# Attention followed by an expert layer on one core: a new order for the first three attention units, unread matmuls, and an earlier third expert

## The chip, the cores and the metric

The kernel runs on one core of a Trainium2 chip. Such a core has four engines that compute (TensorE or PE, VectorE or DVE, ScalarE or ACT, GpSimd or POOL), a fifth that only issues transfers (SyncE or SP), and 16 DMA engines that all queues share. Each engine works through its own instructions in the order in which they stand in the program, and waits on semaphores where it needs another's result. The metric is the device time of one execution in microseconds; several executions are timed and the median is compared.

## What is computed

The reference, cut to what matters (B, H, S, D = 4, 8, 768, 64; 8 global and 96 local positions; 3072 tokens of 512, 8 experts, F = 1024):

```python
scores = scale * np.matmul(q, k.transpose(0, 1, 3, 2)) + bias   # bias = -slope[h] * distance
scores = np.where(is_global | is_local, scores, -1e9)
a = softmax(scores)
x = matmul(a, v).transpose(0, 2, 1, 3).reshape(B * S, H * D)
logits = x @ w_gate                        # one logit per token and expert
# pairs in falling order of logit: a token takes the expert if it has none yet and the expert is not full (384)
for e in range(8):
    out[assigned == e] = np.maximum(x[assigned == e] @ w1[e], 0) @ w2[e]
```

## The kernel before

**Attention** works on 8 units (half of the heads of one batch, four heads), each of two pairs, a and b. Only a band of 216 queries per block of 120 keys is computed, in seven blocks, which stand in three groups (`GROUPS`, L196). What is done to a unit `u` is cut into named steps, and `step` (L539) issues one. Their names are those of the lists, with the unit after the colon:

- KT0, KT1, QT0, QT1: VectorE transposes half of k or q in blocks of 32 (`blocks`, L276) into one of four buffers `tT`. When both halves are done, the load of a later unit follows on SP (q of u+2 or k of u+3) into one of five raw slots.
- KB: ScalarE copies most of a k half to `kA` (`kA_big`, L284); KS: GpSimd copies the rest. QO: ScalarE, in some places VectorE, copies a q half to `qT` (`qT_out`, L299).
- S0, S1, S2: TensorE's scores of a group (L335). The PSUM they write is used again by the next group, so they wait for the biases of the one before. S1 of unit 0 uses spare banks.
- BI0a to BI2b: VectorE adds the bias (`bias`, L342), two instructions a step. EX: ScalarE takes the exponential (L360). M0, M1: GpSimd adds the overlapping parts (`merge`, L365). AV0, AV1: TensorE multiplies with v (`attend`, L384). OT: ScalarE copies the result out. SU: TensorE's sums and logits (`sums`, L403). LT, GT, LS: VectorE and GpSimd finish sums and logits. TK, TO: rows of x are transposed back and scaled. WT: a piece of the weights of the first two experts is loaded (`weight_piece`, L316).

The order is written out by hand. `ORDER` (L528) is one period in which steps of up to four units stand interleaved, and it is run through under `manual_schedule`, in which every engine's order is the program's. Ahead of it stands a prologue of `steps(...)` lines (L613 to L657) for what can't follow the period: unit 0, most of unit 1, the constants (`consts_`) and the first loads. `done` keeps a step from being issued twice.

**Routing** (`routing`, L707) finds the experts' tokens in four rounds (`fast_round`, L770) and then the two lists of indices (`dispatch`, L846). In the gaps, rows of x that are left are transposed on TensorE (`rows`, L745), scaled on ScalarE (L507) and written to `x_tok` in DRAM on SP. `fill` (L729) issues matmuls that nobody reads. Weights of the later experts are loaded by `late_weights` (L692) from GpSimd: one piece at the start of the routing and one in each of three rounds, the others in the experts' loop. A piece is a whole w1 or w2, 1 MB.

**Experts** (`experts`, L1044): for each expert three slabs of 128 tokens are gathered (L1057), transposed (`load_x`, L1063), multiplied with w1 (`hidden`, L1075, ScalarE's relu at L1082) and w2 (L1107), copied from PSUM by VectorE (L1110) and scattered to `out` (L1111). Expert 0 does slab 0 by itself and slabs 1 and 2 together. Here the order within an engine is the scheduler's, save for what is pinned by `keep_in_program_order`.

## Time and profile before

| | us |
|---|---|
| median of 3 runs | 273.35 (271.0 to 273.55) |
| the profiled execution | 269.57 |
| its span, first to last instruction | 267.9 |
| PE busy | 232.1 (87%) |
| DVE, ACT, POOL busy | 150.5, 153.5, 153.3 (56 to 57%) |

A row of the timeline has start and duration in us, the engine, the line of the kernel, the operation, output <- inputs, shapes and the number of instructions merged into it, and in brackets how long the engine was idle before and what released it. The releaser is inferred, and can be wrong where a wait is for several things. PEclk is TensorE's granted clock as a share of 2.4 GHz; 0.5 is 1.2 GHz. In the page's slices it stands in tenths.

### The profile page before, as it was taken

How to read it: one execution, taken by the hardware profiler on the slowest of the kernel's cores; microseconds unless marked ns; L12 is line 12 of the kernel's file. 1: busy time of each engine (PE TensorE's matmuls, PEld its weight loads, DVE VectorE, ACT ScalarE, POOL GpSimd, SP SyncE). 2: the span in 40 equal slices, each digit the busy share in tenths (PEclk: the TensorE clock that was granted, in tenths of full speed). 3: DMA queues.
4: the chain of work that ended last, by engine and by line, in shares of the span. 5: the costliest groups of instructions: out<-in, count | busy, mean ns of one | idle time of the engine just before them, and what ended most of it. 6: DMA issues, size and time to landing. Idle time of an engine off the chain costs nothing. (4 is left out here: it accounts for less than half of the span.)

```text
span 267.9 us, 6769 instructions
## 1 busy us (share of the span) xinstructions
PE 232.1 (87%) x2681; PEld 164.4 (61%) x2681; DVE 150.5 (56%) x332; ACT 153.5 (57%) x304; POOL 153.3 (57%) x283
## 2 busy tenths in 40 slices
PE   0675599999998999999878888999999989999960
PEld 0654478888886888878657651956555545555520
DVE  3699678879998976564787772132321412323130
ACT  2549658999989999645678860525235051432500
POOL 6878734749585989968311004757565564741240
PEclk9997579999999999999999995899999999999995
DMA  6998976675455399990699991599999999330221
GB/s 246 339 356 214 269 291 190 151 225 125 134 111 111 56 183 206 191 216 7 97 180 220 241 299 48 109 218 244 243 267 240 268 238 303 131 138 36 84 91 37
DMA packets 49862, 49.22 MB, mean 184 GB/s; under 512 B 29344, under 2 KB 41376, under 8 KB 49824
## 3 DMA queue, kind: packets, MB, share of 16 engines
q0 software_dynamic: 15680, 26.22, 46.6%
q1 hardware_dynamic: 34144, 22.50, 30.4%
q8 instruction: 23, 0.38, 0.6%
q14 instruction: 15, 0.12, 0.1%
HBM read 56.05 MB, written 9.44 MB: 244 GB/s over the span
## 5 line engine op out<-in xcount | busy, mean ns | idle before, releaser
L1082 ACT ACTIVATE hT<-ph 128x384 bf16<-128x384 f32 (+2 forms) x72 | 32.6, 454 | 62.5 <-PE ph L1079 60.9
L335 PE MATMUL ps<-qT,kA 32*128 32x216 f32 (+2 forms) x864 | 47.9, 358 | 15.0 <-POOL wgx L635 9.3
L353 DVE SCALAR_TENSOR_TENSOR P<-Dm,ps 128x432 f32<-128x432 f32 x92 | 49.2, 595 | 13.9 <-PE ps L335 13.8
L335 PEld LDWEIGHTS ps<-qT,kA 32*128 32x128 f32 x864 | 40.6, 200 | 20.1 <-POOL wgx L635 9.3
L372 POOL TENSOR_TENSOR S<-P 128x576 f32<-128x576 f32 (+1 forms) x32 | 39.0, 1218 | 19.9 <-ACT P L360 14.8
L360 ACT ACTIVATE P<-P 128x864 f32<-128x864 f32 x48 | 42.6, 923 | 13.5 <-DVE P L353 12.7
L393 PE MATMUL po<-P,v 128*64 128x216 f32 (+6 forms) x576 | 43.3, 299 | 2.9 <-ACT P L360 2.7
L393 PEld LDWEIGHTS po<-P,v 128*64 128x64 f32 x576 | 36.0, 139 | 12.5 <-ACT P L360 3.4
L1111 POOL DMA_INDIRECT out_dram<-ot,ido x24 | 23.6, 984 | 28.5 <-DVE ot L1110 25.3
L1057 POOL DMA_INDIRECT xe<-x_tok,idi x24 | 23.3, 969 | 26.8 <-PE pw L732 18.6
L1110 DVE COPY ot<-po 128x512 f32<-128x512 f32 x24 | 16.4, 691 | 30.9 <-PE po L1107 24.4
L1107 PEld LDWEIGHTS <-hT 128*128 128x128 bf16 x192 | 18.2, 98 | 19.2
L1073 DVE COPY xT<-pxe 128x512 bf16<-128x512 bf16 x24 | 9.5, 422 | 35.8 <-PE pxe L1070 35.0
L507 ACT ACTIVATE x<-pw,ri 128x64 bf16<-128x64 f32 x112 | 24.6, 363 | 5.7 <-PE pw L492 5.4
L286 ACT COPY kA<-tT_k 128x720 f32<-128x720 f32 (+2 forms) x18 | 23.9, 1339 | 5.5 <-DVE tT_k L278 5.5
L1107 PE MATMUL po<-w_late,hT 128*128 128x512 bf16 x96 | 22.0, 379 | 0.0
L1079 PE MATMUL ph<-xT,w_late 128*128 128x384 bf16 x128 | 21.5, 326 | 0.0
L400 ACT COPY oT<-po 128x384 f32<-128x384 f32 x32 | 14.5, 477 | 11.8 <-PE po L393 11.8
L303 ACT COPY qT<-tT_q 128x768 f32<-128x768 f32 (+1 forms) x13 | 19.7, 1512 | 0.6 <-DVE tT_q L278 0.6
L278 DVE STREAM_TRANSPOSE tT_k<-w_early 128x768 f32<-128x768 f32 x16 | 15.3, 969 | 6.6 <-DMA w_early<-in_k_dram 3.5
L1079 PEld LDWEIGHTS <-w_late 128*128 128x128 bf16 x128 | 12.5, 98 | 8.7
L278 DVE STREAM_TRANSPOSE tT_q<-w_early 128x768 f32<-128x768 f32 x16 | 14.9, 944 | 0.2 <-DMA w_early<-in_q_dram 0.2
(166 smaller groups left out, 309.2 us busy)
## 6 DMA issues: line engine op xcount, KB each, us to landing
w_late<-in_moe_w_dram POOLq DMA_DIRECT2D x8, 1024.0 KB, 11.9
w_early<-in_k_dram SPq DMA_DIRECT2D x8, 768.0 KB
w_early<-in_q_dram SPq DMA_DIRECT2D x8, 768.0 KB
v<-in_v_dram SPq DMA_DIRECT2D x32, 180.0 KB
w_early<-in_moe_w_dram POOLq DMA_DIRECT2D x8, 512.0 KB, 8.9
w_last<-in_moe_w_dram POOLq DMA_DIRECT2D x4, 1024.0 KB, 12.6
x_tok<-x SPq DMA_DIRECT2D x2, 768.0 KB
x_tok<-x SPq DMA_DIRECT2D x2, 384.0 KB
```

The lines of the kernel that those rows point to most:

```text
L278: nc.vector.transpose(out=t, in_=raws[kind, u][:, :, 32 * g : 32 * g + 32])
L286: nc.scalar.copy(out=kAs[u % 2][:, g, i0:i1, 8:128].rearrange("p i (c j) -> p i c j", j=NJ), in_=t[:, i0 * NC5 : i1 * NC5, :].rearrange("p ...
L335: nc.tensor.matmul(at(a)[:, o : o + w], lhsT=kA[r, gd, i, :], rhs=qTt[r, gd, KT * i : KT * i + w], start=(gd == 0), stop=(gd == 1), skip_g ...
L353: nc.vector.scalar_tensor_tensor(out=Ps[n][:, 2 * g : 2 * g + 2, t, :], in0=W, scalar=-8.0 * slopes[2 * (n % NPAIR) + t], in1=st[:, 0 : 2 ...
L360: nc.scalar.activation(P, P, AF.Exp, scale=0.125)
L372: nc.gpsimd.tensor_tensor(out=to[:, :, :, 0:OV], in0=P[:, i0 : i0 + m, :, 0:OV], in1=P[:, i0 - 1 : i0 + m - 1, :, KT:QW], op=ALU.add)
L393: nc.tensor.matmul(po[n, bank][64 * t : 64 * t + 64, a - QB * bank : z - QB * bank], lhsT=v7[:, t, i, :], rhs=Ps[n][:, min(i, 5), t, a - q ...
L507: nc.scalar.activation(x[:, 2 * hf + i, 128 * jj + 64 * t : 128 * jj + 64 * t + 64], ps[:, i, 64 * t : 64 * t + 64], AF.Identity, scale=ri ...
L1079: nc.tensor.matmul(ph[:, 128 * t0 : 128 * t1], lhsT=w1_of(e)[:, kc, 128 * fc : 128 * fc + 128], rhs=xT_of[e][:, kc, t0:t1, :].rearrange("p ...
L1082: nc.scalar.activation(hT[:, fc, 128 * t0 : 128 * t1], ph[:, 128 * t0 : 128 * t1], AF.Relu)
L1107: nc.tensor.matmul(po, lhsT=hT[:, fc, 128 * t : 128 * t + 128], rhs=w2_of(e)[:, fc, :], start=(fc == 0), stop=(fc == NFC - 1))
L1111: s = nc.gpsimd.indirect_dma_start(out=out[:, :], out_offset=bass.IndirectOffsetOnAxis(ap=ido[:, TSLAB * e + t : TSLAB * e + t + 1], axis= ...
```

## The change

It does this:

- The prologue of `steps` lines is replaced by one list, `PROLOGUE`, which holds units 0 to 2, nearly all of 3 and parts of 4 and 5. From unit 4 the period is as it was.
- `warm(24)`: 24 matmuls of 128 x 512 in one accumulation group, whose result is not read, stand first on TensorE.
- The four `tT` buffers and one of the two `qT` buffers become parts of one tile, `arena`. After the last use, w1 and w2 of expert 2 are loaded into it, issued at step GTa of unit 6; there are then 10 late pieces for 12.
- In the routing two late pieces are issued (rounds 0 and 1) for four; one more comes between the gathers of experts 0 and 1.
- In `dispatch` the last rows of x come before the one-hot matrices are built, fills are put into one accumulation group per call, there are 4 + 6 + 8 + 6 of them for 4 + 2 + 8, and the matmul `pf` stands ahead of the last six.
- Expert 0 goes slab by slab, with its TensorE instructions pinned in program order. Of the last output slab ScalarE copies three quarters, VectorE one.

```diff
+    arena = wpool.tile([128, 2 * (4 * NJ * 32 + 2 * S_)], BF16)
+    w1_next = arena[:, 0:WL].rearrange("p (k f) -> p k f", k=NKC)
+    w2_next = arena[:, WL : 2 * WL].rearrange("p (k f) -> p k f", k=NFC)
...
-            t = ttp.tile([128, NJ, 32], FP32, tag="tT", name=f"tT_{kind}{u}_{g}")
+            m = 2 * NJ * 32 * (len(tTs) % 4)
+            t = arena[:, m : m + 2 * NJ * 32].bitcast(FP32).rearrange("p (j c) -> p j c", c=32)
...
+        PROLOGUE = (
+            "KT0:0 KS0:0 KT1:0 QT0:0 QT1:0 KB1:0 QO0:0 WT:1 KP0:0 KS1:0 QP1:0 KB0:0 KP1:0 C12:0 KT1:1 QP0:0 QO1:0 "
+            "KT0:1 KB1:1 KS1:1 QT0:1 WG:0 S0:0 QT1:1 S1:0 KB0:1 BI0b:0 BI0a:0 QO1:1 S2:0 EX0a:0 BI1a:0 QO0:1 "
+            "BI2a:0 KS0:1 EX1a:0 BI2b:0 EX0b:0 AV0a:0 EX2a:0 KT0:2 S0:1 C10:0 OT0a:0 KT1:2 BI0a:1 AV1a:0 EX2b:0 "
+            "C0:0 KB1:2 C11:0 BI0b:1 M0a:0 BI1b:0 OT1a:0 KS1:2 QT1:2 S1:1 KB0:2 EX1b:0 M1a:0 KS0:2 C15:0 BI1a:1 "
+            "C6:0 M0b:0 BI1b:1 QO1:2 SUa:0 AV0b:0 EX1a:1 S2:1 EX0a:1 QT0:2 QT1:3 QO0:2 BI2b:1 BI2a:1 C1:0 AV1b:0 "
...
+            "GTa:1 LTb:1 BI2a:3 EX1b:3 GTb:1 LTa:2 C14:0 LS:1 QO1:4 AV1b:2 EX1a:3 OT1b:2 KT1:5 TKa:2 KB0:5 M0a:3 "
+            "TOa:2 SUb:2 GTa:2 EX2a:3 BI2b:3 LTb:2 M1a:3 "
+        ).split()
+        VLOAD = {"S0:0": 1, "S1:0": 2, "S2:0": 3}
...
+        def warm(n):
+            i = len(warms) % 2
+            t = ps_t.tile([128, 512], FP32, tag=f"t{i}", name=f"warm{len(warms)}")
+            warms.append(t)
+            for m in range(n):
+                nc.tensor.matmul(t, lhsT=ones_bf, rhs=ones_bf.rearrange("p (o n) -> p o n", o=1).to_broadcast([128, 4, 128]),
+                                 start=(m == 0), stop=(m == n - 1))
...
+            elif k == "KP":
+                kA_big(0, int(op[2]), 0, 2)
+            elif k == "QP":
+                qT_out(0, int(op[2]), 0, 14, dve=op == "QP1")
...
-                qT_out(u, int(op[2]))
+                qT_out(u, int(op[2]), 0 if u else 14, dve=u < 2)
...
+                if n == 2 * NU - 4:
+                    nc.gpsimd.dma_start(w1_next, moe_w1[W_EARLY].rearrange("(kc p) f -> p kc f", p=128))
+                    nc.gpsimd.dma_start(w2_next, moe_w2[W_EARLY].rearrange("(fc p) d -> p fc d", p=128))
...
+            warm(24)
...
-            for _ in range(n):
-                pw = ps_d.tile([128, 512], FP32, tag="pk", name="pw")
-                nc.tensor.matmul(pw, lhsT=ident_bf, rhs=w1_early[:, 0, 0, 0:512], start=True, stop=True)
+            pw = ps_d.tile([128, 512], FP32, tag="pk", name="pw")
+            for i in range(n):
+                nc.tensor.matmul(pw, lhsT=ident_bf, rhs=w1_early[:, 0, 0, 0:512], start=(i == 0), stop=(i == n - 1))
...
-            if kk < len(ROUND_KS) - 1:
+            if kk < 2:
                 nc.gpsimd.tensor_copy(out=turn, in_=Xe[:, 0:1])
                 late_weights(False)
...
             rows(2)
             fill(4)
+            rows(2)
+            fill(6)
...
-                if q4 == 1:
-                    rows(2)
...
-            fill(2)
             pO = ps_d.tile([128, NCHUNK], FP32, tag="pr", name="pO")
             for c in range(NCHUNK):
+                if c % 6 == 0:
+                    fill(2)
                 nc.tensor.matmul(pO, lhsT=ohls[c // 6][:, :, c % 6], rhs=OH[:, :, c],
                                  start=(c == 0), stop=(c == NCHUNK - 1))
-            fill(8)
+            pf = ps_d.tile([1, CE], FP32, tag="pr2", name="pf")
+            nc.tensor.matmul(pf, lhsT=ones_bf[:, 0:1], rhs=Mf, start=True, stop=True)
+            fill(6)
...
-            late_weights(False)
             rows(2)
...
+            def first_hidden(hT, t):
+                for f2 in range(NFC // 2):
+                    if f2 == 2 and t + 1 < TSLAB:
+                        load_x(0, (t + 1,))
+                    ph = ps_h.tile([128, CAP], FP32, tag="ph")
+                    for j in range(2):
+                        fc = 2 * f2 + j
+                        for kc in range(NKC):
+                            pin(0, nc.tensor.matmul(ph[:, 128 * j : 128 * j + 128],
...
             gather(0)
+            if first:
+                late_weights()
             gather(1)
...
-                    hidden(0, hT, 0, 1)
-                    load_x(0, range(1, TSLAB))
-                    hidden(0, hT, 1, TSLAB)
+                    for t in range(TSLAB):
+                        first_hidden(hT, t)
...
+                    cuts = (0, DM) if e < N_EXP - 1 or t < TSLAB - 1 else (0, 3 * DM // 4, DM)
...
+                        copy = nc.vector.tensor_copy if hi == DM else nc.scalar.copy
```

## Rows read from the trace of the kernel before

**Rows 1.** The page's slices of 6.7 us: TensorE's granted clock in tenths

```profile
PEclk9997579999999999999999995899999999999995
```

**Rows 2.** Windows, one period of attention: stretch, length, busy us of each engine, clock, DMA

```profile
50.60:63.70 13.10, 12.99 (x235) 10.78 (x234) 10.73 (x22) 12.18 (x15) 8.66 (x18) 1.00 0.70 189
```

**Rows 3.** Timeline of TensorE, 8 to 70 us: scores of S0:0, S1:1, S2:1, S1:3, S0:4

```profile
9.32 3.26 PE L335 MATMUL ps<-qT,kA 32*128 32x216 f32 x32 [9.32 <-POOL wgx L635]
...
30.65 3.26 PE L335 MATMUL ps<-qT,kA 32*128 32x216 f32 x32 [2.95 <-DVE P L353]
...
37.53 1.96 PE L335 MATMUL ps<-qT,kA 32*128 32x216 f32 x48
...
59.11 1.74 PE L335 MATMUL ps<-qT,kA 32*128 32x216 f32 x32
...
68.12 1.98 PE L335 MATMUL ps<-qT,kA 32*128 32x216 f32 x32
```

**Rows 4.** Timeline of VectorE, 5 to 31 us

```profile
5.32 1.84 DVE L278 STREAM_TRANSPOSE tT_k<-w_early 128x768 f32<-128x768 f32 x2 [3.51 <-DMA w_early<-in_k_dram]
7.39 1.84 DVE L278 STREAM_TRANSPOSE tT_q<-w_early 128x768 f32<-128x768 f32 x2 [0.23 <-DMA w_early<-in_q_dram]
...
9.26 1.42 DVE L303 COPY qT<-tT_q 128x336 f32<-128x336 f32 x3
...
28.38 2.12 DVE L353 SCALAR_TENSOR_TENSOR P<-Dm,ps 128x432 f32<-128x432 f32 x4
```

**Rows 5.** Timeline of ScalarE, 7 to 11 us: copies of unit 0

```profile
7.19 0.62 ACT L286 COPY kA<-tT_k 128x240 f32<-128x240 f32 x1 [0.23 <-DVE tT_k L278]
8.40 0.77 ACT L303 COPY qT<-tT_q 128x336 f32<-128x336 f32 x1 [0.59 <-DVE tT_q L278]
9.08 2.00 ACT L286 COPY kA<-tT_k 128x480 f32<-128x480 f32 x2
```

**Rows 6.** Timeline of GpSimd, 121 to 129 us: the last units, a late piece's issue

```profile
121.64 1.01 POOL L372 TENSOR_TENSOR S<-P 128x384 f32<-128x384 f32 x1 [2.88 <-ACT P L360]
...
128.35 0.81 POOL L699 DMA_DIRECT2D w_late<-in_moe_w_dram  x1 [0.65 <-issue]
```

**Rows 7.** The tile x_tok: its writes (duration ns min/median/max, first and last start us)

```profile
L522 SPq DMA_DIRECT2D x_tok<-x x7: 359/360/467, 118.0 to 158.8; - x7
```

**Rows 8.** Windows of 1 us as in rows 2: DMA share and GB/s last

```profile
161.00:162.00 1.00, 0.89 (x3) 0.21 (x2) 0.15 (x1) 0.00 (x0) 0.00 (x0) 0.50 0.12 39
```

**Rows 9.** Timeline, 154 to 176 us: the routing's end and expert 0

```profile
154.55 1.68 PE L732 MATMUL pw<-w_early,ident_bf 128*128 128x512 bf16 x4
...
157.84 0.93 ACT L507 ACTIVATE x<-pw,ri 128x64 bf16<-128x64 f32 x4 [0.62 <-PE pw L492]
...
159.44 1.27 PE L901 MATMUL pO<-OH,ohl 128*128 128x24 f16 x24
...
160.55 5.08 PE L732 MATMUL pw<-w_early,ident_bf 128*128 128x512 bf16 x8
...
163.18 1.08 POOL L1057 DMA_INDIRECT xe<-x_tok,idi  x1 [18.62 <-PE pw L732]
...
166.32 0.58 PE L1070 MATMUL pxe<-ident_bf,xe 128*128 128x128 bf16 x4 [0.44 <-DVE fc L1039]
...
167.47 3.10 PE L1079 MATMUL ph<-xT,w_early 128*128 128x128 bf16 x32 [0.57 <-DVE xT L1073]
...
171.75 3.66 PE L1079 MATMUL ph<-xT,w_early 128*128 128x256 bf16 x32
```

**Rows 10.** Timeline, 180 to 260 us: expert 1's start, a stall, the last eviction

```profile
180.22 1.95 PE L1079 MATMUL ph<-xT,w_early 128*128 128x384 bf16 x11
...
219.82 0.77 PE L1070 MATMUL pxe<-ident_bf,xe 128*128 128x128 bf16 x8 [1.03 <-DMA xe<-x_tok,idi]
...
221.08 4.91 PE L1107 MATMUL po<-w_late,hT 128*128 128x512 bf16 x22
...
258.55 0.69 DVE L1110 COPY ot<-po 128x512 f32<-128x512 f32 x1 [1.04 <-PE po L1107]
```

More of the change, by code (lines that the diff above doesn't have):

```diff
@@ L625 @@
             load("k", 2)
-            steps("KT0 KT1")
-            for g in range(2):
-                kA_big(0, g, 0, 2)
-                kA_small(0, g)
-            steps("QT0 QT1")
-            qT_out(0, 0, 0, 14)
-            qT_out(0, 1, 0, 14, dve=True)
-            consts_(0, 2)
-            for t in range(2):
-                nc.gpsimd.tensor_scalar(out=wgx[64 * t : 64 * t + 64, :, 8 * t : 8 * t + 8],
-                                        in0=wg_sb[64 * t : 64 * t + 64], scalar1=LSCALE, scalar2=None, op0=ALU.mult)
-            consts_(11, 12, 13)
-            load_v(1)
-            steps("S0")
-            for g in range(2):
-                kA_big(0, g, 2)
-                qT_out(0, g, 14, 32, dve=True)
-            for g in range(2):
-                done.update([(f"KB{g}", 0), (f"KS{g}", 0), (f"QO{g}", 0)])
-            steps("BI0a BI0b EX0a")
-            load_v(2)
-            steps("S1")
-            steps("KT0 KS0", 1)
-            steps("BI1a BI1b")
-            consts_(14, 3)
-            steps("KB0", 1)
-            steps("EX1a")
-            steps("KT1 KS1 QT0", 1)
-            load_v(3)
-            consts_(1, 6)
-            steps("S2 BI2a EX2a M0a M1a")
-            qT_out(1, 0, dve=True)
-            done.add(("QO0", 1))
-            steps("QT1", 1)
-            steps("BI2b")
-            steps("KB1", 1)
-            qT_out(1, 1, dve=True)
-            done.add(("QO1", 1))
-            steps("EX0b AV0a OT0a AV1a OT1a EX1b EX2b M0b")
-            consts_(5, 10, 15, 16)
+            for o in PROLOGUE:
+                op, u = o.split(":")
+                if o in VLOAD:
+                    load_v(VLOAD[o])
+                step(op, int(u))
             it0 = 1 + stage["S0"]
@@ L670 @@
                     step(op, it - stage[op])
-            assert len(done) >= NU * len(ORDER), len(done)
+            assert all((o.split(":")[0], u) in done for o in ORDER for u in range(NU))
             while wpieces:
@@ L1034, in routing @@
             rows_out(d0, nc.vector)
[L1035 to L1037 removed]
+            pf = dispatch()
             fc8 = dap.tile([1, N_EXP], FP32)
```

81 lines of the change are left out of this document (47 added, 34 removed), and 6 rows, old and new, of the table PROLOGUE.

## The prediction

> **What bounds the kernel now.** I read the page first. Over the whole span TensorE is busy most, but the clock line has two dips, one around 20 to 40 us and one around 160 to 170 us, where the granted clock is 0.5, the lower of its two levels (1.2 GHz); elsewhere it is 2.4 GHz [rows 1]. So the span falls into stages with different limits, and each is read by itself.
>
> The windows come next. In a steady unit of attention TensorE is busy 12.99 of 13.10 us and ScalarE 12.18, at full clock: TensorE sets the pace there and ScalarE is close behind [rows 2]. What comes out of order in the first units is therefore not made up later, and what is gained there is kept to the end of attention.
>
> The timeline shows what the first units lose. TensorE's first scores S0:0 start at 9.32, S1:1 at 30.65 and S2:1 at 37.53, and from there to S0:4 at 68.12 it runs on with hardly a gap. At the lower clock 32 score matmuls take 3.26 us, at the higher one 1.74 [rows 3]; S0:0's 3.26 says that TensorE was at the lower one there too, where the clock line, which has only the changes, shows full clock. On VectorE the transposes, q copies and biases of these units follow each other almost without a gap: biases BI0a:1 and BI0b:1 end at 30.5, and S1:1, which needs the PSUM that they read, starts 0.15 us after [rows 3, 4]. VectorE's order sets this stage, with TensorE's clock on top. The routing is a chain of small steps that this diff touches only at its end; expert stage and tail are TensorE's.
>
> **The change part by part.**
>
> *1. The order of the first three units.* I walk VectorE's new queue with the old durations [rows 4]. A transpose is 0.92 us (1.84 for two), a bias step 1.06 (2.12 for two: four instructions), and a q copy goes by columns: 336 + 432 + 432 took 1.42, so 0.40, 0.51 and, for all 768, 0.91. The four transposes of unit 0 are where they were (until 9.23, since q lands at 7.39). Then: QO0:0, QP1:0, KT1:1, QO1:0, KT0:1, QT0:1, QT1:1 = 0.51+0.40+0.92+0.51+3x0.92 = 5.10; BI0b:0, BI0a:0 2.12; QO1:1 0.91; BI1a:0 1.06; QO0:1 0.91; BI2a:0, BI2b:0 2.12; KT0:2, KT1:2 1.84; BI0a:1, BI0b:1 2.12. Together 16.2 us from 9.26, so they end at 25.4 where they ended at 30.5.
>
> Does anything make VectorE wait in it? ScalarE now copies KB1, KP0, KB0, KP1, QP0 from 7.19 on: 1.00+0.62+1.00+0.62+0.77 = 4.0, so S0:0 starts at 11.2 instead of 9.3 [rows 5]. It ends at 12.9 (14.5 at the lower clock); BI0b:0 comes up at 14.4. S1:0 has banks of its own; S2:0 follows BI0a:0 (16.5) and ends at 18.4, and BI2a:0 comes up at 19.3. S0:1 follows BI2b:0 (21.5), ends at 23.2, and BI0a:1 comes up at 23.3. So at full clock each score is done just in time, and at the lower one each costs up to 1.5 us. The loads: q0 was there 2.07 us after k0's first use [rows 4], so k1 and q1, next in the queue, should be there at about 9.5 and 11.6 (estimated); they are wanted at 10.2 and 12.5. The loads that SP now issues earlier (q3, k4 ahead of v) have 5 us and more.
>
> S1:1 then starts at 25.5, 5.1 us earlier. Up to S2:1 TensorE has S1:1 1.74, a sums step of some 1.1 and an attend step of some 1.2, VectorE BI1b:0, QT1:2, BI1a:1, BI1b:1 = 4.1: S2:1 starts at 29.7 against 37.53, 7.8 earlier. (The old stretch of 6.9 us was those same TensorE steps at half clock.) From S2:1 to S0:4 both orders hold the same TensorE work, 30.6 us [rows 3]. I do not expect all 7.8 to last: the new list puts BI2b:3, for which S0:4 waits, behind LTa:2 and TOa:2, which wait for TensorE steps after S2:3, and ScalarE has under 1 us per unit to spare [rows 2]. I take 1.6 back, so 6.2; bounds 4.6 and 7.8. GpSimd's constants are only reordered, and its merges keep a lead of over 1 us on the sums. The arena replaces two pools with the same number of buffers: nothing.
>
> *2. The unread matmuls ahead of the scores.* 24 of 512 columns in one accumulation group. The nearest row is 22 matmuls of 512 columns in 4.91, 0.223 each [rows 10]; at half the clock 512 columns are 0.427 (worked out). They take 5.4 to 10.2 us from when `ones_bf` is written, and end before or about when S0:0 can start (11.2), so they cost nothing. What they buy is S0:0 at full clock, for which the walk has cover anyway, and a chance that the clock stays up. In the walk TensorE still has idle gaps of 1 to 2 us from 14.6 to 25, and the old trace shows the clock falling in such a patch. Price: between 0 and 4.4 us (S0:1 and S1:1 1.5 each, attend and sums some 1.4). Since the new queue is denser, I take 1.0. Part 1 and 2 together: 5.2 us earlier at the end of attention.
>
> A rule speaks against counting more. The Trainium skill, "TensorE: Matmul & The Clock Gate", Part 1, says that the ramp is worth under 1% of a typical kernel's span and that one should not fit to it, which here would be under 2.7 us. The rows show more: 1.52 us lost in S1:1 alone, and the clock line has some 13 us at the lower clock in that dip [rows 1]. By that rule I would take about 2 us off the gain (268.4); the rows are what I go by.
>
> *3. Third expert's weights in the last unit.* Two more issues on GpSimd, some 0.81 us each, land behind GTa:6, where GpSimd stood idle 2.88 us waiting for ScalarE [rows 6]: hidden. Their own wait, for the last readers of the arena (unit 6's scores, unit 7's copies), is over a unit earlier. Without that cover they would delay a merge by up to 1.7 us, of which the sums behind it have little to spare. In the routing two pieces of 1 MB remain of four.
>
> *4. The end of the routing.* The last write of x_tok is issued at 158.8, after the last four ACT copies end at 158.77; bytes hardly move after 161.2; the first gather starts at 163.18 [rows 7 to 9]. The last rows now come up before ACT has worked off the 32 before them, so its 0.62 us of idle time goes: 0.6. The transfer itself loses its competition: of the 2.4 us from issue to last byte I take 1.0 (0 to 1.9); the 2.0 us after the last byte stays. Gather 1.6 earlier. Beside it TensorE: pO started at 159.44; 1.27 for it, 14 fills and some 0.3 for pf. At 0.223 a fill it is done at 164.2, at 0.427 at 167.0; by the gather the transposes could start at 164.7, against 166.32 [rows 9]. I take 165.0: 1.3 earlier (+0.7 to -1.6).
>
> *5. Expert 0 by slabs.* From the first transposes to expert 1's first matmul it was 13.9 us [rows 9, 10]. The 96 matmuls of 128 columns stand against 32 + 32 wider ones (3.10 + 3.66). Half of the old first slab ran at the lower clock, 0.097 each; at the higher one a quarter of 0.223 would be 0.056 by columns [rows 9, 10]. So 5.4 to 9.3 us for 6.8: I take no change (-0.9 to +2.0). A weight issue now stands between gathers 0 and 1 on GpSimd; gather 1 is wanted 11 us later.
>
> *6. The last weights* start one piece earlier. There was one stall, 1.03 us at 219.8, on a gather [rows 10]. The same eight pieces still stand around it; I count nothing (1.0 either way).
>
> *7. The tail.* The last eviction took 0.69 us [rows 10]. Three quarters move to ScalarE beside the last eight short matmuls; the remaining quarter is some 0.2 to 0.3: 0.4 less (0 to 0.5).
>
> **Sum.** 5.2 + 1.3 + 0.4 = 6.9 us. The profiled execution took 269.57 (span 267.9 and 1.7 around it), so 262.7 there; the runs' median is 273.35, 3.8 above the profiled one, and I take the difference off that: 266.4. Own range, by the terms' bounds: 263 to 270.
>
> **The rivals.**
> *B, the clock falls and stays down in the first units.* The gaps speak for it, the denser queue against it. It costs 4.4 in place of 1.0, so attention ends only 1.8 earlier, and the routing's end and tail give perhaps 0.7: 270.9.
> *C, slower: the unread matmuls take their latency and not their columns.* For: the old fills did, 4 in 1.68 (0.42) and, at the lower clock, 8 in 5.08 (0.635) [rows 9]. Against: each of those began a new tile, and matmuls of one group go at 0.223. At 0.635 the 24 take 15.2 us, S0:0 slips from 11.2 to some 16.5 and BI0b:0 by 3.9, which leaves 1.3 of the 5.2; fourteen fills take 8.9, so expert 0's transposes start at 169.9, 3.6 later than before; the slabs at the lower clock add 1.0. With the tail it is 2.9 slower: 276.2. It turns the sign from about 0.53 us a matmul (6.9 us over 38 matmuls at the forecast's mean of some 0.35).
>
> **How the numbers follow.** Forecast 0.74, B 0.18, C 0.08. A measurement of this kernel can tell about 1%, 2.7 us: faster means under 270.6. The forecast gives 0.72 faster and 0.02 within; B lies across that bound, 0.06 and 0.12; C gives 0.01 within and 0.07 slower. Range 261.5 to 271.8: it takes in the forecast, a stall of 1.0 us saved beside its best bounds, and most of B.
>
> **What would show it.** Right: S0:0 near 11 us, S1:1 near 25.5, S2:1 near 30, S0:4 near 62; the granted clock at 1.0 from 25 us on; the end of attention 5 us earlier; DMA busy in the last unit and less so before the gather; first gather some 2 us after the last bytes and near 156.5. Wrong: a clock of 0.5 through 25 to 37 us (B); unread matmuls more than 0.45 apart, or TensorE still on fills when the first gather lands (C); VectorE idle before KT1:1 or QT0:1 (loads late); or the first expert's slabs taking over 9 us.

## The result, and the profile after

| | before | after |
|---|---|---|
| median, timed side by side, us | 272.33 (271.0 to 273.55, 4 runs) | 268.69 (266.75 to 270.22, 4 runs) |
| ratio, 95% interval | | 0.9871 (0.9825 to 0.9917) |
| the profiled execution, us | 269.57 | 268.25 |
| its span, us | 267.9 | 266.4 |
| mean granted clock | 0.945 | 0.974 |

The change makes the kernel 3.6 us faster (1.3%); 6.9 were forecast. The two profiled executions are only 1.5 us apart in span: the one of before took less than any timed run of before. So the rows below are read against each other for where time went, and the size of the gain is taken from the medians. A ratio here and below leaves out runs that took over 1.5% more than the kernel's fastest; for rows_first_from_1 that is three of six.

First the start. The page's line of the granted clock, in 40 slices and tenths, then the timeline: TensorE from 0 to 70 us (the unread matmuls; scores S0:0, S2:0, S1:1, S2:1; S0:3 in two pieces; S0:4) and ScalarE's first row copies behind the attention at 125.68:

```profile
PEclk9979999999999999999999998999999999999995
```

```profile
1.21 8.15 PE L566 MATMUL warm<-ones_bf 128*128 128x512 bf16 x24 [1.21 <-POOL ones_bf L71]
11.12 1.74 PE L341 MATMUL ps<-arena,kA 32*128 32x216 f32 x32 [1.77 <-ACT arena L309]
...
16.23 2.84 PE L341 MATMUL ps<-arena,kA 32*128 32x216 f32 x48 [1.91 <-DVE P L359]
...
24.38 2.50 PE L341 MATMUL ps<-qT,kA 32*128 32x216 f32 x32
...
29.13 1.96 PE L341 MATMUL ps<-qT,kA 32*128 32x216 f32 x48
...
46.62 1.36 PE L341 MATMUL ps<-qT,kA 32*128 32x216 f32 x19
48.84 1.00 PE L341 MATMUL ps<-qT,kA 32*128 32x216 f32 x13 [0.86 <-issue]
...
63.04 2.32 PE L341 MATMUL ps<-arena,kA 32*128 32x216 f32 x32
...
125.68 1.75 ACT L513 ACTIVATE x<-pw,ri 128x64 bf16<-128x64 f32 x8 [1.92 <-PE pw L498]
```

The wide dip at 20 to 40 us [rows 1] is gone. S1:1 comes 6.3 and S2:1 8.4 us earlier than in [rows 3], S0:4 only 5.1. In between, S0:3 loses 1.5 us: 3.22 from start to end where 32 such matmuls take 1.74, with a gap of 0.86 us behind its 19th matmul for which the trace names no other engine ("issue"). The row copies came at 129.87 before: the attention ends 4.2 us earlier.

Windows of the lapse of the clock that is left there (stretch, length, busy us of PE, PEld, DVE, ACT, POOL, clock, DMA share, GB/s), and of a second one in expert 0. The DMA share adds up the times of all packets, so it can pass 1:

```profile
16.00:17.00 1.00, 0.77 (x16) 0.80 (x20) 1.00 (x3) 0.88 (x1) 0.00 (x0) 1.00 0.99 406
17.00:18.00 1.00, 1.00 (x24) 1.00 (x20) 1.00 (x3) 0.15 (x2) 0.38 (x1) 0.57 1.03 424
18.00:20.00 2.00, 2.00 (x29) 1.66 (x24) 1.52 (x3) 1.63 (x2) 1.10 (x1) 0.50 1.05 423
20.00:21.00 1.00, 1.00 (x14) 0.72 (x12) 1.00 (x3) 0.77 (x1) 0.56 (x2) 0.73 0.98 260
...
164.00:167.00 3.00, 3.00 (x31) 3.00 (x29) 0.42 (x1) 1.17 (x4) 2.39 (x4) 0.50 0.94 146
```

The end of the routing and expert 0, from the timeline (last write of x_tok, the last fills, first gather, expert 0's transposes, its first and last matmuls with w1, expert 1's start):

```profile
153.88 0.36 SPq L528 DMA_DIRECT2D x_tok<-x  x1
...
157.70 1.47 PE L740 MATMUL pw<-w_early,ident_bf 128*128 128x512 bf16 x6
...
158.52 1.08 POOL L1066 DMA_INDIRECT xe<-x_tok,idi  x1 [23.48 <-DVE fm L1050]
...
162.26 0.38 PE L1079 MATMUL pxe<-ident_bf,xe 128*128 128x128 bf16 x4 [3.09 <-issue]
...
163.22 1.26 PE L1094 MATMUL ph<-xT,w_early 128*128 128x128 bf16 x16 [0.57 <-DVE xT L1080]
...
171.34 0.61 PE L1094 MATMUL ph<-xT,w_early 128*128 128x128 bf16 x8 [0.88 <-issue]
...
178.46 5.36 PE L1104 MATMUL ph<-xT,w_early 128*128 128x384 bf16 x32
```

Against [rows 7, 9]: last write 4.9 us earlier, first gather 4.7, transposes 4.1, but expert 1 [rows 10] only 1.8. Expert 0 takes 16.2 us for 13.9. TensorE has done its fills at 159.2 and stands 3.1 us until the transposes of the first rows at 162.3, 3.7 us after their gather's start (2.9 to 3.2 in all other kernels here); behind that its clock falls. The first late piece asked for behind the first gather, in the kernel before (first line) and in the changed one, then in the changed one the stall ahead of expert 5, expert 5's start, and the tail:

```profile
170.55 0.85 POOL L699 DMA_DIRECT2D w_late<-in_moe_w_dram  x1
```

```profile
162.16 0.87 POOL L707 DMA_DIRECT2D w_late<-in_moe_w_dram  x1
...
218.49 0.77 PE L1079 MATMUL pxe<-ident_bf,xe 128*128 128x128 bf16 x8 [1.46 <-DMA xe<-x_tok,idi]
...
224.50 5.36 PE L1104 MATMUL ph<-xT,w_late 128*128 128x384 bf16 x32
...
256.79 0.48 ACT L1141 COPY ot<-po 128x384 f32<-128x384 f32 x1 [4.26 <-PE po L1138]
257.24 0.29 DVE L1141 COPY ot<-po 128x128 f32<-128x128 f32 x1 [1.05 <-PE po L1138]
258.30 0.97 POOL L1142 DMA_INDIRECT out_dram<-ot,ido  x1 [0.87 <-DVEq L1162]
```

So of 4.7 us at the first gather 1.5 are left at the end. Two questions follow: why the gather came at 158.5 and not near 156.5, and why what lies behind it became 3.2 us longer.

### The profile page after: what moved, and what is told of

It is laid out like the page before. It is cut to its first block, busy times and chain, and to the rows that moved or that the text cites. A ratio compares the mean times of both kernels' runs of the same rounds, so it can differ in the third digit from the quotient of the medians.

```text
span 266.4 us, 6908 instructions
## 1 busy us (share of the span) xinstructions
PE 236.4 (89%) x2745; PEld 167.1 (63%) x2755; DVE 149.4 (56%) x332; ACT 153.5 (58%) x301; POOL 152.6 (57%) x282
## 4 chain that ended last, share of the span: by engine, by line
PE 65%; DMA 11%; DVE 11%; issue 5%; ACT 4%; POOLq 1%; POOL 1%; DVEq 0%; ACTq 0%
PE ps L341 15%; PE po L399 14%; PE po L1138 11%; PE ph L1104 8%; DMA xe<-x_tok,idi 5%; DMA w_last<-in_moe_w_dram 5%; PE t L416 4%; PE ph L1094 3%; DVE P L359 3%; ACT x L513 2%; DVE arena L281 2%; PE pw L740 2%; PE t L420 2%; DMA w_early<-in_k_dram 2%; PE pxe L1079 2%
## 5 line engine op out<-in xcount | busy, mean ns | idle before, releaser
L1107 ACT ACTIVATE hT<-ph 128x384 bf16<-128x384 f32 x56 | 27.5, 491 | 51.7 <-PE ph L1104 50.0
L1141 DVE COPY ot<-po 128x512 f32<-128x512 f32 (+1 forms) x24 | 16.2, 675 | 32.6 <-PE po L1138 29.7
L281 DVE STREAM_TRANSPOSE arena<-w_early 128x768 f32<-128x768 f32 x32 | 29.8, 953 | 5.0 <-DMA w_early<-in_k_dram 3.6
L289 ACT COPY kA<-arena 128x720 f32<-128x720 f32 (+2 forms) x18 | 23.7, 1345 | 5.9 <-DVE arena L281 5.8
L341 PE MATMUL ps<-arena,kA 32*128 32x216 f32 (+2 forms) x416 | 21.7, 343 | 5.4 <-DVE P L359 2.5
L341 PE MATMUL ps<-qT,kA 32*128 32x216 f32 (+2 forms) x448 | 24.1, 335 | 2.0 <-DVE P L359 1.0
L341 PEld LDWEIGHTS ps<-arena,kA 32*128 32x128 f32 x416 | 18.7, 194 | 7.7 <-issue 5.0
L341 PEld LDWEIGHTS ps<-qT,kA 32*128 32x128 f32 x448 | 20.0, 184 | 4.6 <-issue 2.5
L406 ACT COPY oT<-po 128x384 f32<-128x384 f32 x32 | 14.7, 476 | 11.6 <-PE po L399 11.5
L1138 PE MATMUL po<-w_late,hT 128*128 128x512 bf16 x69 | 15.9, 379 | 0.0
L416 PE MATMUL t<-S,onesx 128*32 128x192 f32 x256 | 13.7, 332 | 0.0
```

What stands on the lines that cost most here:

```text
L281: nc.vector.transpose(out=t, in_=raws[kind, u][:, :, 32 * g : 32 * g + 32])
L289: nc.scalar.copy(out=kAs[u % 2][:, g, i0:i1, 8:128].rearrange("p i (c j) -> p i c j", j=NJ), in_=t[:, i0 * NC5 : i1 * NC5, :].rearrange("p ...
L341: nc.tensor.matmul(at(a)[:, o : o + w], lhsT=kA[r, gd, i, :], rhs=qTt[r, gd, KT * i : KT * i + w], start=(gd == 0), stop=(gd == 1), skip_g ...
L416: nc.tensor.matmul(pr[32 * gq : 32 * gq + 32, :], lhsT=onesx[:, t, :], rhs=S[:, t, 192 * gq : 192 * gq + 192], start=(t == 0), stop=True, ...
L1107: nc.scalar.activation(hT[:, fc, :], ph, AF.Relu)
L1138: pin(e, nc.tensor.matmul(po[:, lo:hi], lhsT=hT[:, fc, 128 * t : 128 * t + 128], rhs=w2_of(e)[:, fc, lo:hi], start=(fc == 0), stop=(fc == ...
```

## The experiments

Each kernel was timed beside the kernel before, whose medians ranged from 269.1 to 272.3 with the chip and the hour; so ratios and places in the trace are compared, and medians only between kernels that ran together. "To the end" is from the first gather to the end of the span; spans and places are of the profiled executions. Six kernels have the same program up to the end of the attention (changed, e0_whole, third_late, tiny16, rows_first_6, best_tiny); their first row copies behind it came between 123.9 and 125.7 us, the changed kernel's last of all. So a place in a single trace is uncertain by about 1 us either way.

| kernel | ratio (95%) | span | first gather | expert 1 | expert 5 | to the end |
|---|---|---|---|---|---|---|
| before | 1 | 267.9 | 163.18 | 180.22 | 225.83 | 104.7 |
| changed | 0.9871 (0.9825 to 0.9917) | 266.4 | 158.52 | 178.46 | 224.50 | 107.9 |
| e0_whole | 0.9833 (0.9788 to 0.9878) | 265.2 | 157.33 | 175.33 | 223.11 | 107.9 |
| no_warm | 0.9769 (0.9722 to 0.9817) | 264.1 | 156.31 | 174.34 | 222.03 | 107.8 |
| old_order | 0.9960 (0.9927 to 0.9992) | 268.7 | 160.69 | 179.05 | 226.69 | 108.0 |
| third_late | 0.9885 (0.9830 to 0.9940) | 266.6 | 158.56 | 179.37 | 224.67 | 108.0 |
| tiny16 | 0.9898 (0.9870 to 0.9926) | 264.9 | 156.73 | 173.18 | 222.94 | 108.2 |
| no_warm_tiny24 | 0.9911 (0.9885 to 0.9937) | 267.0 | 156.93 | 174.64 | 225.05 | 110.1 |
| no_warm_w_after | 0.9940 (0.9919 to 0.9962) | 266.3 | 155.93 | 172.36 | 224.24 | 110.4 |
| no_warm_whole_w | 0.9919 (0.9889 to 0.9949) | 266.0 | 156.46 | 172.30 | 223.95 | 109.5 |
| rows_first_6 | 0.9979 (0.9945 to 1.0013) | 268.9 | 157.77 | 181.49 | 226.96 | 111.1 |
| rows_first_from_1 | 0.9706 (0.9645 to 0.9766) | 262.1 | 154.65 | 172.78 | 218.07 | 107.4 |

### The start: the order and the unread matmuls

**old_order** puts the prologue's old lines back and keeps the rest.

```diff
-            for o in PROLOGUE:
-                ...
+            steps("KT0 KT1")
+            ...
```

> The changed kernel with the order of the first units as it was (unread matmuls kept). Theory: the new order is worth the attention's 4 to 5 us: S2:1 goes back to 36 to 37.5, the last sums end 4 to 5 us later, and the kernel is 3.5 to 5 us slower than the changed one, so some 1 us slower than the one before. Rival: the start sets only part, since the later units wait for VectorE anyway (S1:5 and S1:4 stood 0.6 to 1.0 us on it): 1 to 2.5 us slower.

S2:1 starts at 35.59 (6.5 later than in the changed kernel), S0:4 at 66.18 (3.1 later), the row copies at 127.96 (2.3 later), and the span ends 2.3 later. S2:1 in the trace shows the start; what remains of it at the end of attention is the rival's 1 to 2.5. Against the mean of the six kernels with the new order and the unread matmuls (124.8) the row copies are 3.2 later. So the order is what makes most of the kernel's gain (0.9960 without it, 0.9871 with it), but half to two thirds of its 6.5 us are lost again before the attention ends.

**no_warm** leaves out the unread matmuls.

```diff
-            warm(24)
```

> The changed kernel without the 24 unread matmuls ahead of the first scores. Theory (the prediction's step 2): they lie in time that TensorE has free and bring S0:0 to full clock; without them S0:0 starts near 11 and takes 3 to 3.5 us instead of 1.74, S2:1 starts 0 to 1.5 later, the kernel is 0 to 1.5 us slower. Rival: they delay the first scores and buy the lapse of the clock at 17 to 20.5 us, so that without them S2:1 is not later and the kernel is 0.5 to 2 us faster.

It is faster, and by more than the rival said: 0.9769 against 0.9871. TensorE's timeline (S0:0, S2:0, S1:1, S2:1, S0:3) and GpSimd's first gather in this kernel:

```profile
11.02 3.26 PE L341 MATMUL ps<-arena,kA 32*128 32x216 f32 x32 [11.02 <-ACT arena L309]
16.66 1.96 PE L341 MATMUL ps<-arena,kA 32*128 32x216 f32 x48 [0.79 <-DVE P L359]
...
24.26 2.50 PE L341 MATMUL ps<-qT,kA 32*128 32x216 f32 x32
29.01 1.96 PE L341 MATMUL ps<-qT,kA 32*128 32x216 f32 x48
...
45.96 1.74 PE L341 MATMUL ps<-qT,kA 32*128 32x216 f32 x32
...
156.31 1.08 POOL L1065 DMA_INDIRECT xe<-x_tok,idi  x1 [21.82 <-PE pw L739]
```

S0:0 takes 3.26 instead of 1.74, and nothing follows from it: S1:1 and S2:1 start 0.1 us *earlier*, because VectorE sets the scores ahead of them. The lapse at 17 to 21 us isn't there either: five of the six kernels with the new order and the unread matmuls have a stretch at 0.5 somewhere between 11.6 and 20.9 us (e0_whole has none), none of the six without them has. The gap in S0:3 is gone. It stands behind the same 19th matmul in all six kernels that have the new order and the unread matmuls (0.30 to 0.86 us), and there in none of the six that have the new order without them; S0:4 starts 1.2 us later with them (mean of six 62.3 against 61.1). In each of the six it ends 2.6 to 2.8 us after a packet of the instruction queue starts (what that is comes in the next section). Two of the other six have such a gap further on (no_warm 0.37 us up to 56.74, no_warm_tiny24 0.79 up to 49.77), 2.7 and 2.9 us behind such a packet. That fits TensorE waiting for its own instructions; no run tests it. By the row copies the 1.2 us are levelled out (124.8 against 124.6). The rows where no_warm really gains are at the gather: its last write of x_tok goes out at 153.32, so the gather follows it by 2.99 us, for 4.64 in the changed kernel; the other 0.6 us of the 2.2 are the earlier write.

### The first gather: a packet of the instruction queue

The DMA traffic of that stretch, GB/s in 40 slices of 0.15 us each from 153 to 159 us: the changed kernel, then no_warm.

```profile
GB/s 103 27 20 0 0 0 0 0 0 0 0 48 410 348 328 307 287 21 0 0 0 14 7 14 7 27 20 21 0 0 0 0 0 0 0 0 0 0 0 0
```

```profile
GB/s 0 0 0 0 0 0 0 0 287 348 341 341 335 96 0 0 0 0 0 0 0 0 0 109 0 0 0 0 0 0 0 0 0 0 300 109 300 164 0 0
```

In the changed kernel the last x_tok transfer has a tail: its last 17 packets come one by one, the last of them 1.5 us after the rest. In no_warm there is no tail; a single packet (109) stands alone at 156.5. The DMA view by queue names it. Queue, packets, MB, share of 16 engines; the changed kernel at 154.75 to 155.0, then no_warm at 156.5 to 156.75:

```profile
q8 instruction: 1, 0.02, 34.6%
```

```profile
q8 instruction: 1, 0.02, 30.6%
```

It is one packet of 16 KB of some engine's instructions, and it takes 1.2 to 1.4 us of one DMA engine (0.31 to 0.35 of 16 engines for 0.25 us). In the changed kernel it falls on the transfer's start. The Trainium skill, "Runtime: NRT & Kernel Launch", "Instruction fetch mechanics", says that each engine's instructions are fetched in blocks of 16 KiB, 256 instructions, by DMA, and that a block's cost is mostly hidden. The packet's size agrees; that it is hidden doesn't hold here. By the size of a block, 24 matmuls with their weight loads, 48 instructions, would move such a packet along TensorE's program. Two kernels test that, with 16 or 24 matmuls of 8 columns (two instructions each) in the routing rounds, where TensorE waits (tiny16 as below; no_warm_tiny24 with `tiny(6)` and without `warm(24)`):

```diff
+        def tiny(n):
+            pw = ps_d.tile([128, 512], FP32, tag="pk", name="pw")
+            for i in range(n):
+                nc.tensor.matmul(pw[:, 0:8], lhsT=ident_bf, rhs=ident_bf[:, 0:8], start=(i == 0), stop=(i == n - 1))
...
                                     start=(k1 == 0), stop=(k1 == k - 1))
+            tiny(4)
```

> The changed kernel with 16 unread matmuls of 8 columns added, four in each of the four routing rounds, where TensorE waits for VectorE. They add 32 instructions to TensorE's stream and nothing that anything waits for. Theory: the changed kernel's first gather starts 4.64 us after the issue of the last x_tok (2.95 without the unread matmuls at the start) because one 16 KB packet of the instruction queue falls into that transfer at 154.8 us, and 16 or 17 packets of x_tok come 1.5 us behind the rest; where that packet falls follows TensorE's place in its instructions. With 32 more instructions ahead it falls before the transfer: the gather starts 2.7 to 3.2 us after the last issue and the kernel is 1 to 2 us faster than the changed one. Rival: the gather waits for the reductions behind the dispatch (its releaser by the profile, fm), which nothing here moves: 4.3 to 4.9 us as before, the same time plus or minus 0.5.

> The changed kernel without the 24 unread matmuls at the start, and 24 unread matmuls of 8 columns in the routing rounds (six in each): at the dispatch TensorE's stream has as many instructions behind it as in the changed kernel. Theory (the packet of the instruction queue): it falls into the last x_tok transfer again, the first gather starts 4.3 to 4.9 us after the last issue, and of the 3.2 us that leaving out the unread matmuls gained 1 to 2 are lost (266.5 to 267.5). Rival: the whole gain is of the start (clock, the gap in S0:3): the gather 2.7 to 3.2 us after the last issue, 265.0 to 266.2.

The same GB/s line from 152 to 158 us, tiny16 and then no_warm_tiny24:

```profile
GB/s 355 246 34 0 0 0 0 109 0 0 0 0 0 198 314 355 348 335 123 14 27 20 14 0 0 0 0 0 0 0 0 0 0 0 0 0 0 0 0 0
```

```profile
GB/s 0 0 0 0 205 423 335 348 321 116 0 0 0 0 0 0 7 7 7 14 7 27 20 21 0 0 0 0 0 0 0 0 0 0 0 0 0 0 0 0
```

In tiny16 the packet (109) has moved ahead of the transfer, and only a short tail is left right behind the transfer; in no_warm_tiny24 it is back on top of the transfer, with the tail. From the last write's issue to the first gather:

| packet | kernels | us |
|---|---|---|
| behind the transfer | no_warm, no_warm_w_after, no_warm_whole_w, rows_first_from_1, best_cold | 2.99 each |
| ahead of it (16 small matmuls) | tiny16, best_tiny | 3.62, 3.68 |
| on it, or on its end | changed, old_order, rows_first_6, no_warm_tiny24, e0_whole, third_late | 4.5 to 5.2 |

The releaser that the timeline prints (fm, in the rival) was wrong: nothing about fm was moved. In all 14 traces the gather starts 1.2 to 1.3 us after the last packet of that write has ended; it waits for the write. The kernel before is no exception: there, too, such a packet stands in the write (at 161.05, the 130 in its GB/s line from 158 to 164 us, slices of 0.15 us), and the write's last packet ends at 161.98, behind a tail:

```profile
GB/s 423 341 382 341 376 342 396 369 396 287 219 369 362 389 355 362 225 232 109 34 130 27 20 27 20 27 7 0 0 0 0 0 0 0 0 0 0 0 0 0
```

So the unread matmuls did cost 1.6 us at the gather, 145 us behind the place where they stand, by moving the packet. At the end tiny16 shows less than the 1 to 2 us that were expected. Its span is 1.5 us shorter than the changed kernel's (264.9), but by the ratio it is no faster (0.9898 against 0.9871, the intervals overlap). no_warm_tiny24 lost all that no_warm had gained (0.9911 against 0.9769); part of that is a stall and a fall of the clock near expert 5. The next part says what becomes of time won at the gather.

### Behind the first gather: what the experts' stage is bound by

**e0_whole** puts expert 0's old order back.

```diff
-                    for t in range(TSLAB):
-                        first_hidden(hT, t)
+                    hidden(0, hT, 0, 1)
+                    load_x(0, range(1, TSLAB))
+                    hidden(0, hT, 1, TSLAB)
```

> The changed kernel with expert 0 alone put back (slab 0, then both others at once, no pinning of po). In the changed kernel's trace expert 0 took 16.2 us from its first transposes to expert 1's first ph, in the one before 13.9. Theory 1, the slab order and the pinning cost 2.3 us: expert 0 takes 13.5 to 14.3 again, expert 1's first ph comes near 176.2 and the kernel is 1.5 to 2.5 us faster than the changed one (266 to 267). Rival, the loss is the halved clock of 164 to 167 us, which follows from TensorE's idle 159.2 to 162.3 whatever the order: expert 0 takes 15.5 to 16.5 and the time stays within 0.7 us of the changed kernel's 268.7.

Neither. Expert 0 takes 15.0 us, and expert 1 starts 3.1 us earlier than in the changed kernel; but the end comes only 1.2 earlier, just what the first gather does. TensorE's timeline in e0_whole (starts of experts 1 and 4, two stalls, start of expert 5):

```profile
175.33 5.36 PE L1088 MATMUL ph<-xT,w_early 128*128 128x384 bf16 x32
...
204.26 0.76 PE L1079 MATMUL pxe<-ident_bf,xe 128*128 128x128 bf16 x8 [1.43 <-DMA xe<-x_tok,idi]
...
210.27 5.36 PE L1088 MATMUL ph<-xT,w_late 128*128 128x384 bf16 x32
217.13 0.75 PE L1079 MATMUL pxe<-ident_bf,xe 128*128 128x128 bf16 x8 [1.49 <-DMA xe<-x_tok,idi]
...
223.11 2.11 PE L1088 MATMUL ph<-xT,w_late 128*128 128x384 bf16 x12
```

What expert 0 won is stood out again at 204 and 217, waiting for gathered rows. tiny16 shows it more strongly: expert 1 starts at 173.18, 5.3 earlier, with three such stalls (1.65, 1.47, 1.49), and expert 5 only 1.6 earlier. Six kernels have the late pieces and gathers in one order. In five (changed, e0_whole, no_warm, tiny16, old_order) expert 5 starts 62.1 to 62.6 us after GpSimd asks for the first late piece (162.16, 160.97, 159.95, 160.36, 164.29), while expert 1 starts anywhere from 12.8 to 16.3 us after it. (In the sixth, no_warm_tiny24, it is 64.5: behind its stall of 1.88 us the clock falls, and 22 matmuls of 512 columns take 6.06 us for 4.91 [rows 10].) In the changed kernel the DMA engines have a share of 1.04 to 1.23 in every stretch of 5 us from 165 to 215 us: expert 5's start is theirs, and TensorE's work between is hidden in it. Eight late pieces are asked for ahead of expert 5's rows here, and from the first one's issue to the transposes of these rows it is 56.3 us (162.16 to 218.49). Before, there were seven, and it was 49.3 us (170.55 to 219.82 [rows 10]): 7.04 us a piece in both.

**third_late** asks for the third expert's weights in the routing stage again, and for the first late piece behind both gathers.

```diff
-                if n == 2 * NU - 4:
-                    nc.gpsimd.dma_start(w1_next, ...)
-                    nc.gpsimd.dma_start(w2_next, ...)
...
-            if kk < 2:
+            if kk < len(ROUND_KS) - 1:
...
             gather(0)
-            if first:
-                late_weights()
             gather(1)
```

> The changed kernel with the third expert's weights asked for in the routing stage again, into the same memory. Theory (the prediction's steps 3 and 6): hidden in either place; the last x_tok is set by ScalarE and goes out at 154 plus or minus 0.5, the kernel is 0 to 1 us slower (the experts' later weights land later, the stall of 1.46 us grows). Rival: with the transfers in the routing stage again (DMA share 1.1 there before) the rows of x_tok and the first gather come 1 to 2 us later, and the kernel is 1.5 to 3 us slower.

No difference (266.6 in span), as the theory had it. Seven pieces are asked for ahead of expert 5's rows here, as before, and not eight, but the transposes of these rows start no earlier (218.66 for 218.49). The stall ahead of them is 0.72 instead of 1.46 because TensorE comes 0.9 us later: expert 0 took 17.9 us, with a granted clock of 0.58 and 0.74 in 160 to 165 and 165 to 170 us. So third_late's third piece, which is asked for in expert 1's turn, went out 15.6 us after the first (11.8 in the kernel before), and the DMA share fell to 0.85 in 180 to 185 us.

**no_warm_w_after** and **no_warm_whole_w** move the first late piece behind expert 1's gathers; the second has expert 0's old order as well.

```diff
             gather(0)
+            gather(1)
             if first:
                 late_weights()
-            gather(1)
```

> The changed kernel without the unread matmuls at the start, and with the first late weights asked for after the gathers of expert 1 again, as before, not between those of experts 0 and 1. Theory: in the changed kernel the weights' packets (DMA share over 1 from 163 us) delay the rows of expert 0's last slab, and TensorE stood 1.4 us in expert 0; without that expert 0 takes 13.7 to 14.3 us instead of 15.1, the kernel is 0.5 to 1 us faster than without the unread matmuls alone (265.5). Rival: the late weights end that much later, the stalls ahead of experts 3 and 4 (1.34 and 1.48 us) grow by as much, no gain.

> The same, with expert 0 in the order of before (slab 0, then both others at once, po not pinned). If the order of the slabs costs something of its own, expert 0 takes 13.3 to 13.9 and the kernel is 0.5 to 1.5 us faster than the same with slabs; if the clock and the landing of the rows are all of it, both are within 0.5 us of each other.

Expert 0 takes 13.4 and 12.75 us: the shorter times that were expected, and the pair gives the slabs a price of their own of 0.7 us. Yet both end later than no_warm, by 2.2 and 1.9 us in span. The late pieces start 3.4 and 3.9 us later (163.32 and 163.84 for 159.95), and in whole_w TensorE waits for rows in front of experts 2, 3, 4 and 5 (1.13, 1.68, 1.93, 1.48): the first kernel's rival. By the ratio, too, both are slower than no_warm. Delaying the weights cost more here than expert 0 won by it.

**rows_first_6** tests the turn: rows ahead of weights.

```diff
-                if first:
-                    late_weights()
                 if e + 2 < N_EXP:
                     gather(e + 2)
                 if first:
                     late_weights()
+                    late_weights()
...
             gather(0)
-            if first:
-                late_weights()
             gather(1)
```

> The changed kernel with one thing else: GpSimd asks for the rows of expert e+2 ahead of the two pieces of late weights of expert e's turn, and not for a piece between the gathers of experts 0 and 1. In the changed kernel eight pieces of 1 MB are asked for ahead of the rows of expert 5, here six. Theory: from 163 us the DMA engines are full, what is asked for lands in turn, some 6.9 us for each piece (8 pieces: 163.3 to 218.5; before, 7 pieces: 172 to 219.8), and so expert 5 starts 66.0 us after the first gather whatever expert 0 does (65.7 to 66.2 in six kernels of the changed kind). With six ahead the stall of 1.46 us ahead of expert 5 is gone, expert 5 starts 44.3 us after expert 1 (four periods of 11.07), and the kernel is 1.3 to 2 us faster than the changed one. Rival: the engines are full either way, the rows share them with whatever weights are under way, and the stall stays at 1 to 1.5 us (or moves to a late weight): no change within 0.5.

The stalls on rows are gone, as the theory said: after expert 1 none is left but 1.26 us on a copy. The kernel is slower all the same, since expert 0 now takes 20.8 us. **best_cold** and **best_tiny** put diffs from above together: this one, e0_whole's, and no_warm's or tiny16's.

> Three edits on the changed kernel: no unread matmuls at the start, expert 0 in the order of before, rows ahead of the late weights (six pieces ahead of expert 5's rows). Theory: first gather near 156.3, expert 0 in 12.8 to 13.5 us, expert 1 at 172.3 to 173, and with no stalls expert 5 at 216.6 to 217.5 and a span of 258.5 to 260 (0.96 of before). Rival (the DMA engines' bytes and not their turn set the experts): the end comes 107.9 us after the first gather again, a span of 264 (0.977).

> The same, but with the unread matmuls at the start kept and 16 unread matmuls of 8 columns in the routing rounds, so that the packet of the instruction queue falls ahead of the last x_tok transfer. Theory: the unread matmuls at the start cost 0.5 to 1.5 us by the lapse of the clock and the gap in S0:3, so 0.3 to 1.5 us slower than best_cold; first gather 0 to 0.6 us later. Rival: no difference between the two (under 0.3 us), the attention's end being set elsewhere.

Both miss: 0.9870 (0.9812 to 0.9927) and 0.9999 (0.9966 to 1.0032). The kernel with the unread matmuls is the slower one again, but in the two traces the first gather starts at the same place (156.45 and 156.43), so the packet isn't what parts them, and what does is open. In all three expert 0 takes some 21 us. The view that shows where is VectorE's and GpSimd's timelines, 159 to 171 us, in best_tiny:

```profile
159.88 0.42 DVE L1088 COPY xT<-pxe 128x512 bf16<-128x512 bf16 x1 [2.38 <-PE pxe L1085]
...
166.67 0.95 POOL L1072 DMA_INDIRECT xe<-x_tok,idi  x1 [0.30 <-issue]
167.61 1.81 POOL L707 DMA_DIRECT2D w_late<-in_moe_w_dram  x2
...
169.42 0.76 DVE L1088 COPY xT<-pxe 128x512 bf16<-128x512 bf16 x2 [9.11 <-remote]
```

and in rows_first_6:

```profile
168.92 1.81 POOL L707 DMA_DIRECT2D w_late<-in_moe_w_dram  x2
...
170.65 0.42 DVE L1080 COPY xT<-pxe 128x512 bf16<-128x512 bf16 x1 [6.30 <-remote]
```

The last copy shown on VectorE starts when, or just before, GpSimd ends its run of nine gathers and two weight issues (167.61 + 1.81 = 169.42; 168.92 + 1.81 = 170.73). The brackets give VectorE's idle time; the transposes that it copies had ended at 164.8 and 166.6 us, so the copies came 4.6 and 4.1 us late. Why hand-overs between other engines come late beside such a run wasn't found; that it isn't gathers as such is seen in whole_w, where six in a row went beside 32 matmuls and 8 copies on ScalarE with no gap.

**rows_first_from_1** keeps expert 0's turn and puts the rows first from expert 1's on.

```diff
-                if first:
+                if first and e == 0:
                     late_weights()
                 if e + 2 < N_EXP:
                     gather(e + 2)
                 if first:
                     late_weights()
+                    if e:
+                        late_weights()
```

> The changed kernel without the unread matmuls at the start, and from expert 1's turn on the rows of expert e+2 asked for ahead of both pieces of late weights; expert 0's turn stays as it was, so that GpSimd doesn't issue nine gathers in a row. Seven pieces are ahead of expert 5's rows instead of eight, five ahead of expert 4's instead of six. Theory (what is asked for lands in turn, some 6.9 us a piece): the stalls ahead of experts 3 and 5 (1.34 and 1.48 us without the unread matmuls) go or shrink to under 0.5 us, expert 0 still takes 15 us, from the first gather to the end 105 to 106 us instead of 107.8, 0.967 to 0.973 of before. Rival (the engines' bytes, not their turn): 107.5 to 108 us again, 0.977. Third: nine gathers in a row were not what held up expert 0 in rows_first_6, and it takes 18 us or more here too: 0.985 or above.

Expert 0 takes 15.2 us, so the third possibility is out. No wait on gathered rows is left, as the theory said. But to the end it is 107.4 us, closer to the rival's: ahead of expert 3 TensorE waits 1.09 us for a copy on VectorE, and in expert 5 (TensorE's timeline) it waits for ScalarE:

```profile
218.07 2.11 PE L1103 MATMUL ph<-xT,w_late 128*128 128x384 bf16 x12
222.04 3.41 PE L1103 MATMUL ph<-xT,w_late 128*128 128x384 bf16 x20 [1.86 <-ACT hT L1106]
```

ScalarE got its first block of expert 5 only at 221.50. That is a late hand-over again, behind a run of three gathers and a scatter; its cause is open too. The kernel's ratio is the lowest of all, and its interval lies below the changed kernel's; against no_warm the intervals overlap. Both beat the kernel before and the changed one.

## Why the prediction was right, and where it was not

The sign, the range (261.5 to 271.8) and the side of the 1% bound were right; the time, 266.4, is 2.3 us below the 268.69 that was measured. That the time fell into the range is in part luck: the range is 10 us wide, and of the 6.9 us only 3.6 came. In the traces the first gather won 4.7 us, and 3.2 of them were lost in a stage where the forecast counted nothing.

1. *Order.* Right up to S2:1: S0:0 at 11.1 (11.2 said), S1:1 24.4 (25.5), S2:1 29.1 (29.7). Of the lead over [rows 3], 3.3 us were given back by S0:4, where 1.6 were taken off: 63.0 for 61.9, inside the bounds. 1.5 of it is the gap in S0:3. Of the 8.4 us at S2:1 only 4.2 are left at the row copies (5.2 forecast), so what is gained in the first units is not all kept to the end of the attention, as the prediction took from [rows 2].
2. *Unread matmuls.* Rival C is out: the 24 took 8.15 us, those up to 7 us at about half the pace of the rest (some 6 in 2 us, then 11), and were done at 9.4. Rival B is out: the lapse that was allowed for came, at 17 to 21 us, and ended. That they cost nothing failed too, and in a way that the step didn't look for: not TensorE's time but their number, 48 instructions, which moved a packet of the instruction queue onto the last x_tok transfer. That S0:0 at full clock buys nothing was right. The rule of the Trainium skill, "TensorE: Matmul & The Clock Gate", Part 1, that the ramp is worth under 1% of a typical kernel's span, agrees for the ramp itself: S0:0 lost 1.52 us in no_warm, 0.6% of the span, and none of it reached the end.
3. *Third expert's weights.* Hidden, as said (third_late: 266.6 and 266.4).
4. *Routing's end.* ScalarE's idle time went, and the last write came 4.9 us earlier: right. That "of the 2.4 us from issue to last byte I take 1.0 (0 to 1.9); the 2.0 us after the last byte stays" failed: from issue to gather 4.64, for 4.38 before and 3.4 forecast. The last byte was misread: in the trace of before the write's last packets, behind a packet of the instruction queue, end at 161.98 and not at 161.2, and from there to the gather it is 1.2 us. Without that packet the whole is 2.99. The step saw neither that such a packet stood in the old write nor that one could stand in the new one. The fills were done at 159.2, by their columns.
5. *Expert 0.* "I take no change" was wrong, +2.3, just outside its bound of +2.0. The slabs' own price is 0.7 by the one pair above. The halved clock behind the 3.1 us in which TensorE had no fills left is part of the rest, but not all: the same slabs took 15.1 us in no_warm and 13.4 in tiny16, both at full clock throughout. How the rest divides is open. But e0_whole shows that expert 0 decides little.
6. *The last weights.* This is the step that failed and weighs most. "The same eight pieces still stand around it; I count nothing": eight stand ahead of expert 5's rows now, for seven before, the DMA engines are full from 165 us on, and expert 5's start is set by them. The first piece is asked for 3.64 us after the first gather and not 7.37, which wins 3.7 us, but one more piece of 7.04 us lands ahead of the rows: 3.3 us lost, and the stage is 3.2 us longer. The forecast took each microsecond before that stage as one at the end; among the kernels with this turn, time won ahead of the first gather reached the end only as far as the first late piece went out earlier.
7. *Tail.* The last copy ended 0.38 us earlier after expert 7's start, as forecast (0.4); but the scatter started 0.77 us after it, for 0.28 before, and so no earlier. Nothing was won.

What is open: that the eighth piece is what made the stage longer is worked out from the traces of two kernels, not shown by a run of its own. third_late has seven pieces and the first of them behind both gathers, as before, but its long expert 0 delayed the third piece, and it stays at 108.0 us; e0_whole, with expert 0's old order and eight pieces, stays at 107.9. Both undone together, with the old turn of the weights, wasn't tried.

## What to carry to other kernels

Before counting a gain ahead of a stage, ask what bounds that stage from its first transfer: here, in five kernels with one turn of weights and rows, expert 5 started 62.1 to 62.6 us after the first late weights were asked for, and 4.7 us won in front of the stage were worth 1.5 in span. Where the DMA engines are busy all the time, the turn in which rows and weights are asked for decides who waits, and in two kernels delaying the first weights cost more than it spared. Instructions that nobody waits for still move where the instructions behind them are fetched; if a change shifts time far away from its place, look at the instruction queue's packets there.

## What was not expected of the hardware

- A single 16 KB packet of the instruction queue delayed what waited for a 256 KB write by 1.6 to 2.2 us: 16 of the write's 256 packets of 1 KB came late in five of the six kernels (in third_late other transfers hide it), and in every trace the first gather started 1.2 to 1.3 us after the last packet.
- A gap of 0.30 to 0.86 us that the trace gives to no other engine came at the same matmul in six kernels with the same TensorE program up to it, and was absent there when 48 instructions ahead of it were left out. It ended 2.6 to 2.8 us after the start of an instruction packet each time; its cause wasn't isolated.
- Beside a run of nine gathers and two weight issues on GpSimd a VectorE copy of 0.42 us started 4.6 us after its input was done (4.1 in a second kernel), just when the run ended.
- S0:0 took 3.26 us for 32 matmuls, about half the pace of 1.74, in windows whose granted clock is 1.00 (no_warm, 11 to 15 us): the clock line doesn't show how TensorE starts.
